# Larger loads in a ring of three slots for a decode-attention kernel whose time is set by its transfers

## The chip, the cores and the metric

The kernel runs on one core of one Trainium2 chip. The metric is the device time of a whole execution in microseconds (us). The time before is 402.05 us, the median of three runs (402.03 to 402.28).

In this text PE is the matrix engine, DVE the vector engine, ACT the scalar engine, POOL the general-purpose engine, and SP the engine that issues the large loads. "The 16 engines" are the 16 DMA engines of the core. Each large load is cut by rows (128 partitions, 8 rows per engine), and one packet is one contiguous run of one row.

## The reference

One token goes through attention with a long cache and, beside it, through a small MLP. All large data are bf16.

```python
x  = A_x                                  # (1, 1, 1024)
xn = layernorm(x)
# attention: 32 query heads, 4 KV heads, 65536 keys, Dh 128
q = xn @ wq                               # wq 1024 x 4096
scores = q . k_cache * Dh**-0.5           # k_cache, v_cache (1, 4, 65536, 128)
a = softmax(scores) @ v_cache
a = a.reshape(1, 1, 4096) @ wo            # wo 4096 x 1024
# MLP mixer on xn
h  = gelu(layernorm(xn) @ w1)             # w1 1024 x 1024
hs = (h, its four quarters shifted by 1 or 2 along the sequence) @ w2
x1 = xn + hs
h2 = gelu(layernorm(x1) @ w3) @ w4        # w3 1024 x 3584, w4 3584 x 1024
out = x + a + x1 + h2
```

The kernel reads 169.87 MB, of which K and V are 134.2 MB.

## The kernel before

K and V come in loads of 4 MB (16384 keys, 32 KB per partition), into two slots each. DVE transposes K from its slot into a buffer `X` in pieces of 32x32. The softmax runs over 8192 keys at a time (index `n`), and POOL keeps the running output. Weights share a buffer `W`, or borrow a slot.

```python
W = sb("W", [P, 14336], BF)
X = sb("X", [P, 2, 8192], BF)
Kn = sb("Kn", [P, 2, 16384], BF)
Vn = sb("Vn", [P, 2, 16384], BF)
# ... cut
def issue_kv(t, b_t, cache, m, ch):
    h, nb = divmod(m, NPAIR // HKV)
    s = m % 2
    src = cache[0, h, nb * 2 * SUB:(nb + 1) * 2 * SUB, :].rearrange("(p c) d -> p (c d)", p=P)
    _dma(q_sp, chan("%s%d" % (ch, s)), lambda e: e.dma_start(out=t[:, s, :], in_=src), writes=b_t[s])
# ... cut
def Ttr(n, idx):          # transposes of K, out of place: slot -> X
    s, half = (n // 2) % 2, n % 2
    for ix in idx:
        _op(q_dve, lambda e, ix=ix: e.transpose(out=X32[:, n % 2, 1024 * ix:1024 * (ix + 1)],
                in_=Kn32[:, s, 4096 * half + 1024 * ix:4096 * half + 1024 * (ix + 1)]), ...)
# ... cut
for n in range(NT):       # 32 groups of 8192 keys
    QK(n)
    Ttr(n + 1, [0])       # the next group's K is transposed while this group is worked on
    stats1(n); MB(n); stats2(n); EXP(n)
    Ttr(n + 1, [1])
    PTr(n)
    Ttr(n + 1, [2, 3])
    PV(n); FLASH(n)
    # ... weights: w1, w2, w3, wo, each in W
    if n % 2 == 0: issue_k(n // 2 + 2)
    else:          issue_v(n // 2 + 2)
# w4 comes last, in four loads of 14, 8, 4 and 2 rows per partition
```

The weights' products are made in between, and the last work after the last load is eight matmuls, one copy and a 2 KB store.

## Time and profile before

| | before |
|---|---|
| time, median of three | 402.05 us |
| span in the profile | 400.9 us |
| bytes read | 169.87 MB |
| packets in all | 7087 |
| busy: DMA queue q1 / DVE / PE | 98.6% / 57% / 49% |

The table of windows (columns: stretch, its length, busy time of five engines with instruction counts, PE's granted clock, DMA share, GB/s):

```profile
core 0: us, PE busy (x) PEld busy (x) DVE busy (x) ACT busy (x) POOL busy (x), PEclk, DMA share, GB/s
...
100.00:150.00 50.00, 26.34 (x283) 12.74 (x286) 29.88 (x56) 5.77 (x15) 6.98 (x9) 0.57 1.00 429
...
300.00:350.00 50.00, 24.75 (x208) 8.28 (x212) 34.96 (x55) 7.24 (x19) 7.41 (x9) 0.53 1.00 431
```

A DMA share of 1.00 means that the transfers never pause.

The end of the span, from the timeline (start us, us, engine, line, operation; in brackets the idle time before it and what ended that):

```profile
394.51 1.88 PE L404 MATMUL OUT_ps<-Kn,gh_bf 128*1 128x256 bf16 x32 [1.69 <-DMA Kn<-in_B_w_dram]
...
396.93 1.02 PE L404 MATMUL OUT_ps<-Kn,gh_bf 128*1 128x256 bf16 x16 [0.54 <-DMA Kn<-in_B_w_dram]
...
398.16 0.60 PE L404 MATMUL OUT_ps<-Kn,gh_bf 128*1 128x256 bf16 x8 [0.20 <-DMA Kn<-in_B_w_dram]
398.80 0.42 DVE L631 CAST orow<-OUT_ps 128x256 bf16<-128x256 f32 x1 [13.00 <-PE OUT_ps L404]
399.26 0.65 SPq L632 DMA_DIRECT2D out_dram<-orow  x1
```

The trace also has a record of every packet with start and duration. The medians before are 159 ns for 4 KB, 309 for 8 KB, 611 for 16 KB, 1062 for 28 KB and 1213 for 32 KB.

### The profile page before, as it was taken

How to read it: one execution, taken by the hardware profiler on the slowest of the kernel's cores; microseconds unless marked ns; L12 is line 12 of the kernel's file. 1: busy time of each engine (PE TensorE's matmuls, PEld its weight loads, DVE VectorE, ACT ScalarE, POOL GpSimd, SP SyncE). 2: the span in 40 equal slices, each digit the busy share in tenths (PEclk: the TensorE clock that was granted, in tenths of full speed). 3: DMA queues.
4: the chain of work that ended last, by engine and by line, in shares of the span. 5: the costliest groups of instructions: out<-in, count | busy, mean ns of one | idle time of the engine just before them, and what ended most of it. 6: DMA issues, size and time to landing. Idle time of an engine off the chain costs nothing.

```text
span 400.9 us, 4792 instructions
## 1 busy us (share of the span) xinstructions
PE 194.8 (49%) x1875; PEld 78.5 (20%) x1875; DVE 228.3 (57%) x401; ACT 48.9 (12%) x128; POOL 61.8 (15%) x90
## 2 busy tenths in 40 slices
PE   0432435064525756186541965464443755445655
PEld 0211111021103511062110731121101311111132
DVE  0247475376816588256745287576836775788310
ACT  1000111011101012011110011111201111121100
POOL 5000012012111012011210101111110112112110
PEclk9985656556565566555655555555555655585565
DMA  9999999999999999999999999999999999999994
GB/s 366 451 438 416 427 435 445 418 446 441 417 422 449 436 425 428 432 440 418 433 448 425 420 440 441 422 430 442 418 430 441 445 420 428 423 431 430 443 415 204
DMA packets 7087, 170.19 MB, mean 424 GB/s; under 512 B 916, under 2 KB 920, under 8 KB 1048
## 3 DMA queue, kind: packets, MB, share of 16 engines
q1 hardware_dynamic: 6920, 169.87, 98.6%
q8 instruction: 15, 0.25, 0.2%
q14 instruction: 8, 0.07, 0.0%
q10 hardware_dynamic: 144, 0.00, 0.0%
HBM read 169.87 MB, written 0.00 MB: 424 GB/s over the span
## 4 chain that ended last, share of the span: by engine, by line
DMA 55%; DVE 23%; PE 17%; ACT 2%; issue 2%; POOL 0%; SPq 0%; ACTq 0%
DMA Kn<-in_A_k_cache_dram 44%; DVE X L476 12%; DMA Kn<-in_B_w_dram 6%; DMA Vn<-in_A_wq_dram 5%; PE H_ps L366 4%; PE S_ps L488 3%; DVE pT_f L529 3%; PE OT_ps L536 3%; DVE mrow L495 3%; ACT p_sb L518 2%; PE PT_ps L527 2%; PE M_ps L366 1%; PE M_ps L564 1%; PE OUT_ps L404 1%; DVE Yall L393 1%
## 5 line engine op out<-in xcount | busy, mean ns | idle before, releaser
L476 DVE STREAM_TRANSPOSE X<-Kn 128x1024 f32<-128x1024 f32 x128 | 151.7, 1215 | 67.5 <-DMA Kn<-in_A_k_cache_dram 67.5
L536 PE MATMUL OT_ps<-Vn,pT_f 128*32 128x512 bf16 x512 | 60.7, 627 | 27.2 <-DVE pT_f L529 27.2
L488 PE MATMUL S_ps<-X,Yall 128*32 128x512 bf16 x512 | 58.9, 607 | 16.1 <-DVE X L476 16.1
L501 PE MATMUL MB_ps<-Rm,Lmat 128*128 128x16 bf16 x32 | 6.1, 191 | 90.4 <-DVE Rm L496 90.4
L550 POOL TENSOR_TENSOR O_acc<-O_acc,tmpO 128x513 f32<-128x513 f32 x28 | 32.9, 1174 | 88.4 <-ACT tmpO L544 88.4
L518 ACT ACTIVATE p_sb<-S_ps,brun 128x512 bf16<-128x512 f32 x32 | 22.0, 687 | 192.6 <-DVE brun L516 157.3
L548 POOL TENSOR_SCALAR O_acc<-O_acc,ff 128x513 f32<-128x513 f32 x28 | 19.5, 698 | 153.3 <-ACT ff L523 153.3
L527 PE MATMUL PT_ps<-p_sb,permR 128*128 128x512 bf16 x32 | 17.5, 548 | 38.6 <-ACT p_sb L518 38.6
L495 DVE TENSOR_REDUCE mrow<-S_ps 128x1 f32<-128x512 f32 x32 | 21.6, 674 | 25.5 <-PE S_ps L488 25.5
L544 ACT ACTIVATE tmpO<-OT_ps 128x512 f32<-128x512 f32 x32 | 19.1, 598 | 107.9 <-PE OT_ps L536 107.9
L488 PEld LDWEIGHTS S_ps<-X,Yall 128*32 128x32 bf16 x512 | 16.6, 126 | 54.7 <-DVE X L476 38.2
L529 DVE STREAM_TRANSPOSE pT_f<-PT_ps 128x512 f32<-128x512 f32 x32 | 22.9, 716 | 5.9 <-PE PT_ps L527 5.9
L536 PEld LDWEIGHTS OT_ps<-Vn,pT_f 128*32 128x32 bf16 x512 | 14.5, 129 | 59.0 <-DVE pT_f L529 41.9
L501 PEld LDWEIGHTS MB_ps<-Rm,Lmat 128*128 128x128 bf16 x32 | 3.2, 101 | 115.1 <-DVE Rm L496 115.1
L366 PEld LDWEIGHTS H_ps<-xn_bf,W 128*128 128x128 bf16 x224 | 14.4, 167 | 1.7 <-issue 1.7
L366 PE MATMUL H_ps<-xn_bf,W 128*128 128x1 bf16 x224 | 14.5, 202 | 0.0
L527 PEld LDWEIGHTS PT_ps<-p_sb,permR 128*128 128x128 bf16 x32 | 3.3, 104 | 41.4 <-ACT p_sb L518 41.4
L505 DVE TENSOR_REDUCE Bst<-MB_ps 128x1 f32<-128x16 f32 x32 | 5.5, 173 | 8.3 <-PE MB_ps L501 8.3
L330 PE MATMUL M_ps<-ln_s,ones_f 128*128 128x1 f32 x6 | 1.8, 363 | 16.6 <-DVE ln_s L329 16.6
L546 POOL COPY O_acc<-tmpO 128x513 f32<-128x513 f32 x4 | 2.5, 612 | 47.5 <-ACT tmpO L544 47.5
L404 PE MATMUL OUT_ps<-Kn,gh_bf 128*1 128x256 bf16 x112 | 6.7, 413 | 4.3 <-DMA Kn<-in_B_w_dram 4.3
L631 DVE CAST orow<-OUT_ps 128x256 bf16<-128x256 f32 x1 | 0.4, 425 | 13.0 <-PE OUT_ps L404 13.0
(109 smaller groups left out, 116.4 us busy)
## 6 DMA issues: line engine op xcount, KB each, us to landing
Kn<-in_A_k_cache_dram SPq DMA_DIRECT2D x15, 4096.0 KB, 27.7
Vn<-in_A_v_cache_dram SPq DMA_DIRECT2D x15, 4096.0 KB, 23.1
W<-in_B_w_dram SPq DMA_DIRECT2D x2, 3584.0 KB, 24.9
W<-in_A_wo_dram SPq DMA_DIRECT2D x3, 2048.0 KB, 24.1
Kn<-in_A_wq_dram SPq DMA_DIRECT2D x1, 4096.0 KB, 12.1
Vn<-in_A_wq_dram SPq DMA_DIRECT2D x1, 4096.0 KB, 20.9
W<-in_B_w_dram SPq DMA_DIRECT2D x2, 2048.0 KB, 33.9
Kn<-in_A_k_cache_dram SPq DMA_DIRECT2D x2, 2048.0 KB, 24.9
```

Of the source, the lines that this page charges most:

```text
L366: fns.append(lambda e, j=j, cx=cx: e.matmul(ps_tile[:, c0 + cx:c0 + cx + 1], lhs_fn(j - j0, cx), rhs_fn(j), start=(j == 0 and cx == 0), st ...
L404: fns.append(lambda e, lhs=lhs, rhs=rhs, jj=jj: e.matmul(OUT_ps[32 * jj:32 * jj + 1, 0:256], lhs, rhs[:, 256 * jj:256 * jj + 256], start=F ...
L476: _op(q_dve, lambda e, ix=ix: e.transpose(out=X32[:, xs, 1024 * ix:1024 * (ix + 1)], in_=Kn32[:, s, 4096 * half + 1024 * ix:4096 * half + ...
L488: fns.append(lambda e, we=we, cm=cm, mv=mv: e.matmul(S_ps[32 * cm:32 * cm + 32, :], Yall[:, h, we, :, :].rearrange("p a g -> p (a g)"), mv ...
L495: _op(q_dve, lambda e: e.reduce_max(mrow[:, m:m + 1], S_ps[:, :], axis=AX.X), reads=[b_S], writes=[b_mrow[m]])
L518: _op(q_act, lambda e: e.activation(p_sb[:, m, :], S_ps[:, :], ACTF.Exp, bias=brun[:, kn:kn + 1], scale=SCALE, accum_out=tmpO[:, m, 512:513]),
L527: _op(q_pe, lambda e: e.matmul(PT_ps[:, :], permR[:, :], p_sb[:, m, :], start=True, stop=True), reads=[b_p[m], b_const], writes=[b_PT])
L529: _op(q_dve, lambda e: e.transpose(out=pT_f[:, :], in_=PT_ps[:, :]), reads=[b_PT], writes=[b_pT])
L536: fns.append(lambda e, q=q, q4=q4: e.matmul(OT_ps[32 * q4:32 * q4 + 32, :], pT_bf[:, q, :, 1], Vn[:, s, 8192 * half + 512 * q:8192 * half ...
L544: _op(q_act, lambda e: e.activation(tmpO[:, m, 0:512], OT_ps[:, :], ACTF.Copy), reads=[b_OT], writes=[b_tmpO[m]], partial=True)
L548: _op(q_pool, lambda e: e.tensor_scalar(out=O_acc[:, :], in0=O_acc[:, :], scalar1=ff[:, m:m + 1], scalar2=0.0, op0=ALU.mult, op1=ALU.add), ...
L550: _op(q_pool, lambda e: e.tensor_tensor(out=O_acc[:, :], in0=O_acc[:, :], in1=tmpO[:, m, :], op=ALU.add), reads=[b_tmpO[m]], writes=[b_Oacc])
```

## The change

The intent is to make the large transfers cheaper by making them fewer: fewer packets and fewer loads for the same bytes. To make room, `X`, `W` and the four 32 KB slots become a ring of three slots of 64 KB per partition, K is transposed within its slot, and the small weights' vectors live in the unused end of a slot. A softmax group is 16384 keys, so POOL's running output goes away, and ACT and PE have fewer instructions. `wo` and `w4` are loaded last. The core of the diff, cut:

```diff
-        W = sb("W", [P, 14336], BF)
-        X = sb("X", [P, 2, 8192], BF)
-        Kn = sb("Kn", [P, 2, 16384], BF)
-        Vn = sb("Vn", [P, 2, 16384], BF)
+        KV = sb("KV", [P, 3, SLOT], BF)              # SLOT = 32768 elements = 64 KB
 ...
+        def kv_load(s, ch, src, n, bufs=None):
+            _dma(q_sp, chan(ch), lambda e: e.dma_start(out=KV[:, s, 0:n], in_=src), writes=b_KV[s] if bufs is None else bufs)
 ...
+        kv_load(0, "s0", rows_src(A_wq, 0, 8), 8 * HQD)      # then w1, w2 into slot 1, w3 into slot 2
+        def issue(i):                                # i = 3, 4, ...: K, V, K, V ... of 32768 keys
+                kv_load(slot(i), "s%d" % slot(i), src, SLOT)
 ...
-                _op(q_dve, lambda e, ix=ix: e.transpose(out=X32[...], in_=Kn32[...]), ...)
+                _op(q_dve, lambda e, o=o: e.transpose(out=KV32[:, s, o:o + 1024], in_=KV32[:, s, o:o + 1024]), ...)
 ...
-        w4_parts = [(0, 14, 0, 0), (14, 8, 1, 0), (22, 4, 1, 8), (26, 2, 0, 14)]
+        w4_parts = [(0, 17), (17, 7), (24, 3), (27, 1)]
 ...
+        for m in range(NBLK):                        # 8 blocks of 32768 keys, n = 4 * m
+            Ttr(n, range(4)); QK(n)
+            Ttr(n + 1, range(4)); QK(n + 1)
+            Ttr(n + 2, [0, 1]); MAX(2 * m); Ttr(n + 2, [2]); EXP(2 * m); Ttr(n + 2, [3]); QK(n + 2)
+            PT(n); Ttr(n + 3, [0]); PTr(n); PT(n + 1); Ttr(n + 3, [1]); PTr(n + 1); Ttr(n + 3, [2, 3])
+            PV(n); QK(n + 3)
+            issue(6 + 2 * m)                         # into the slot of this block's K
+            PV(n + 1); MAX(2 * m + 1); EXP(2 * m + 1); FLUSH(2 * m)
+            ...; PV(n + 2); PV(n + 3); FLUSH(2 * m + 1)
+            issue(7 + 2 * m)                         # into the slot of this block's V
```

Before, group n+1's K was transposed while group n was worked on; now a block's transposes begin in the block itself, after the work of the block before is done.

## The prediction

> **What bounds it now.** The transfers. The page's DMA line shows the 16 engines at 90% or more in 39 of 40 slices, and its queue part gives queue q1 98.6% of 16 engines' span: 169.87 MB at 424 GB/s. DVE is busy 57%, PE 49%, ACT 12%, POOL 15% of the span. In the table of windows the DMA share is 0.97 to 1.05 in every 10 us from 10 to 390, so no wait of the queue ever lets an engine run dry; the long SyncE waits (158 us on the PV matmuls) only delay issues that still come in time. The chain of waits agrees: 55% DMA.
>
> Packet records in the trace, medians: 159 ns for 4096 B, 309 for 8192, 611 for 16384, 1062 for 28672, 1213 for 32768. A line of about 27.2 B/ns per engine plus about 9 ns per packet. 16 engines x 27.2 = 435 GB/s; the Trainium skill, "DMA: Bandwidth & Descriptors", section "Where 436 GB/s comes from", states 435.2 GB/s, and the trace agrees. The floor of 169.87 MB is about 390 us. The rest: 6144 data packets x 9 ns / 16 = 3.5 us; 48 loads' closing semaphore writes (9 ns on each engine) 0.4 us; stretched packets 1.3 us; 1.0 us before the first packet; 3.2 us from the last weight byte to the end of the span; 1.1 us between span and reported time.
>
> **What the change does.** Bytes stay the same. Rows of 64 KB per partition halve most packets: 3200 data packets by my count (K, V, wq and wo 64 KB, w3 56 KB, w1 and w2 16 KB). Saved: 2944 x 9 ns / 16 = 1.7 us, plus 22 loads fewer, 0.2 us. The last piece of w4 is one row, so 4 closing matmuls instead of 8 (those 8 took 0.62 us): 0.1 to 0.2 us.
>
> Compute falls (pooled maximum and exponential, no POOL accumulation, wide projections), but none of it sets the time, so I count nothing.
>
> The risk: the ring has three slots of 8.4 MB, 19.3 us each. The K slot of a block is free once its 16 transposes (16 x 1.2 us), the first V matmuls and the last QK are done: an estimate of 25 us after K lands, against 38.7 us until the queue runs dry. The V slot is freed about 33 to 38 us after K lands, with 58 us allowed. In front, wq is used up by 27 us; w1 to w3 keep the queue full until 47; K0 lasts till 66, V0 till 86, and K1 waits only for the gelu, near 58. So no starvation.
>
> **Prediction.** 402.05 - 1.9 - 0.1 = 400.0 us; 399.0 to 401.9. Faster by over 2% (below 394.0) would need more than all of what lies above the byte floor that the change touches: 0.01. Same 0.96, slower 0.03.
>
> **Checks.** Packets fall to about 4000 in all with the 64 KB ones near 2417 ns (16 x 27.2 B/ns again); DMA share stays near 1.0 in each window from 10 to 390 us; last-slice tail unchanged; POOL under 5%, time unmoved by it.
>
> **Wrong if:** Packets split at 32 KB (then about 401.7); 64 KB rows reading memory slower, which shows as packets above 2417 ns; a hole in the DMA share because a slot is freed late, likeliest around the first blocks (40 to 90 us) or at the wo and w4 loads at the end.

## More of the kernel before

The sequence has one position, so each quarter of `h` is shifted out and zeros take its place: `hs` is zero whatever `w1` and `w2` hold.

From the page of the kernel before: busy time of each engine, the busy share of the 16 DMA engines in 40 slices of the span (in tenths), the DMA totals, the large loads' queue, and the chain of waits that ended last.

```profile
PE 194.8 (49%) x1875; PEld 78.5 (20%) x1875; DVE 228.3 (57%) x401; ACT 48.9 (12%) x128; POOL 61.8 (15%) x90
...
DMA  9999999999999999999999999999999999999994
...
DMA packets 7087, 170.19 MB, mean 424 GB/s; under 512 B 916, under 2 KB 920, under 8 KB 1048
...
q1 hardware_dynamic: 6920, 169.87, 98.6%
...
DMA 55%; DVE 23%; PE 17%; ACT 2%; issue 2%; POOL 0%; SPq 0%; ACTq 0%
...
x_bf<-in_A_x_dram ACTq DMA_DIRECT2D x1, 2.0 KB, 12.2
```

The DMA row is what counts: 9 in every slice but the last. No engine that computes is near that. The last line is a DMA issue of another kind: the small load of `x` (2 KB) took 12.2 us from its issue to its landing.

One more view gets its meaning only later, so it is recorded here: DVE's waits in the kernel before (who waited for whom: us in total, times, longest).

```profile
DVE X L476 <- DMA Kn<-in_A_k_cache_dram: 67.5, 11, 9.3
```

DVE stands still for 67.5 us because the next K has not landed yet. That is a first measure of the room that the compute has.

## The result, and the profile after

The changed kernel takes 402.32 us, the median of four runs (401.99 to 402.56). Its ratio to the kernel before is 1.0004 with a 95% interval from 0.9986 to 1.0021: the same. The class was expected, but it says little: the forecast gain of 2.0 us (0.5%) would have been "the same" too. The time lies outside the predicted range of 399.0 to 401.9, and the gain is missing.

The lines of the page after that answer to those of before:

```profile
PE 176.5 (44%) x1611; PEld 70.7 (18%) x1627; DVE 224.5 (56%) x347; ACT 25.2 (6%) x53; POOL 7.1 (2%) x30
...
DMA  9999899999999999999999999999999999999994
...
DMA packets 3770, 170.13 MB, mean 425 GB/s; under 512 B 548, under 2 KB 552, under 8 KB 808
...
q1 hardware_dynamic: 3608, 169.87, 98.4%
...
DMA 41%; DVE 30%; PE 23%; issue 3%; another core or an unknown queue 2%; POOL 0%; SPq 0%; ACT 0%; DVEq 0%
...
KV<-in_A_x_dram ACTq DMA_DIRECT2D x1, 2.0 KB, 22.2
```

The packets are nearly halved (7087 to 3770), POOL and ACT are nearly idle, and the rate over the span is the same 424 to 425 GB/s. The load of `x` lands 10 us later. The chain of waits has less DMA in it and more DVE and PE.

The windows after:

```profile
core 0: us, PE busy (x) PEld busy (x) DVE busy (x) ACT busy (x) POOL busy (x), PEclk, DMA share, GB/s
...
100.00:150.00 50.00, 19.55 (x164) 5.72 (x158) 30.89 (x40) 2.59 (x6) 0.00 (x0) 0.57 1.01 436
...
300.00:350.00 50.00, 19.50 (x158) 7.09 (x156) 32.64 (x42) 2.99 (x6) 0.00 (x0) 0.60 1.00 433
```

The DMA share is 1.00 again: no starvation. DVE's waits for K after:

```profile
DVE KV L436 <- DMA KV<-in_A_k_cache_dram: 8.7, 4, 3.8
```

The room of the compute has shrunk from 67.5 us to 8.7. The end of the span after:

```profile
395.29 0.93 PE L543 MATMUL S_ps<-KV,gh_bf 128*1 128x256 bf16 x28 [2.22 <-DMA KV<-in_B_w_dram]
...
397.18 0.81 PE L543 MATMUL S_ps<-KV,gh_bf 128*1 128x256 bf16 x12 [0.96 <-DMA KV<-in_B_w_dram]
...
398.16 0.38 PE L543 MATMUL S_ps<-KV,gh_bf 128*1 128x256 bf16 x4 [0.16 <-PE S_ps L543]
398.59 0.43 DVE L612 CAST orow<-S_ps 128x256 bf16<-128x256 f32 x1 [15.77 <-PE S_ps L543]
399.05 0.65 SPq L613 DMA_DIRECT2D out_dram<-orow  x1
```

From before to after the last landing of a weight byte moves from 398.11 to 397.80 us, and the store's issue from 399.26 to 399.05.

The packet records of the two traces, worked out:

| | before | after |
|---|---|---|
| K and V packets, data packets in all | 32 KB, 6144 | 64 KB, 3200 |
| their recorded duration, median (ns) | 1213 | 2421 (mean 2431) |
| packets of the same size, first 21 us (ns) | 1213 | 2418 |
| overlap: the next packet starts before the recorded end, by about (ns) | 3.4 | 3.4 |
| sum of all records of queue q1, over 16 engines (us) | 395.27 | 394.36 |
| last landing: earliest and latest of the 16 engines (us) | 394.45 to 398.11 | 394.61 to 397.80 |
| time for 8.39 MB of K or V in the steady stretch (us) | 19.36 | 19.36 |

The last row is the result in one number. Two packets of 32 KB take as long as one of 64 KB, to within 1 ns: an engine does 16 x 1209.6 ns (1213 less the overlap) or 8 x 2420 ns, both 19.36 us. The halved count did not pay, because what one packet costs beyond its bytes rose, by the first two sets of experiments to 1.7 times as much.

### The profile page after: what moved, and what is told of

The parts are those of the page before. It is cut to its first block, busy times and chain, and to the rows that moved or that the text cites. A ratio compares the mean times of both kernels' runs of the same rounds, so it can differ in the third digit from the quotient of the medians.

```text
span 400.7 us, 3966 instructions
## 1 busy us (share of the span) xinstructions
PE 176.5 (44%) x1611; PEld 70.7 (18%) x1627; DVE 224.5 (56%) x347; ACT 25.2 (6%) x53; POOL 7.1 (2%) x30
## 2 busy tenths in 40 slices
DMA packets 3770, 170.13 MB, mean 425 GB/s; under 512 B 548, under 2 KB 552, under 8 KB 808
## 3 DMA queue, kind: packets, MB, share of 16 engines
q1 hardware_dynamic: 3608, 169.87, 98.4%
HBM read 169.87 MB, written 0.00 MB: 424 GB/s over the span
## 4 chain that ended last, share of the span: by engine, by line
DMA 41%; DVE 30%; PE 23%; issue 3%; another core or an unknown queue 2%; POOL 0%; SPq 0%; ACT 0%; DVEq 0%
DMA KV<-in_A_k_cache_dram 29%; DVE KV L436 21%; PE S_ps L448 8%; DMA KV<-in_B_w_dram 7%; DMA KV<-in_A_x_dram 6%; PE OT_ps L492 5%; PE S_ps L385 3%; DVE pT_f L483 2%; PE M_ps L400 2%; DVE mrow L455 2%; PE S_ps L353 1%; PE M_ps L520 1%; DVE Yall L369 1%; PE PT_ps L479 1%
## 5 line engine op out<-in xcount | busy, mean ns | idle before, releaser
L436 DVE STREAM_TRANSPOSE KV<-KV 128x1024 f32<-128x1024 f32 x128 | 148.6, 1210 | 8.8 <-DMA KV<-in_A_k_cache_dram 8.7
L448 PE MATMUL S_ps<-KV,Yall 128*32 128x512 bf16 x512 | 60.7, 622 | 114.5 <-DVE KV L436 114.5
L492 PE MATMUL OT_ps<-KV,pT_f 128*32 128x512 bf16 x512 | 59.3, 612 | 1.3 <-PE OT_ps L492 1.3
L448 PEld LDWEIGHTS S_ps<-KV,Yall 128*32 128x32 bf16 x512 | 16.8, 125 | 148.0 <-DVE KV L436 132.2
L470 ACT ACTIVATE p_sb<-S_ps,brun 128x1024 bf16<-128x1024 f32 x16 | 17.8, 1115 | 281.0 <-DVE brun L468 177.3
L455 DVE TENSOR_REDUCE mrow<-S_ps 128x1 f32<-128x1024 f32 x16 | 19.5, 1216 | 16.8 <-PE S_ps L448 16.7
L479 PE MATMUL PT_ps<-p_sb,permR 128*128 128x512 bf16 x16 | 8.8, 553 | 37.2 <-DVE pT_f L483 37.2
L492 PEld LDWEIGHTS OT_ps<-KV,pT_f 128*32 128x32 bf16 x512 | 17.1, 132 | 35.0 <-issue 33.3
L505 DVE SCALAR_TENSOR_TENSOR O_acc<-O_acc,ff,OT_ps 128x512 f32<-128x512 f32 x12 | 8.9, 744 | 23.6 <-PE OT_ps L492 23.6
L385 PE MATMUL S_ps<-KV 128*32 128x512 bf16 x88 | 12.3, 549 | 2.9 <-DVE KV L333 2.9
```

The costliest lines, as they stand in the source:

```text
L385: fns.append(lambda e, j=j, k=k, mv=mv: e.matmul(S_ps[32 * (k % 4):32 * (k % 4) + 32, bank + k // 4, :], vec[:, j:j + 1].broadcast_to([P, ...
L436: _op(q_dve, lambda e, o=o: e.transpose(out=KV32[:, s, o:o + 1024], in_=KV32[:, s, o:o + 1024]), reads=[b_KV[s][4 * sub + ix]], writes=[b_ ...
L448: fns.append(lambda e, we=we, cm=cm, mv=mv: e.matmul(S_ps[32 * cm:32 * cm + 32, n % 4, :], Yall[:, h, we, :, :].rearrange("p a g -> p (a g ...
L455: _op(q_dve, lambda e: e.reduce_max(mrow[:, k:k + 1], S_ps[:, 2 * k:2 * k + 2, :].rearrange("p b c -> p (b c)"), axis=AX.X), reads=b_S[2 * ...
L470: _op(q_act, lambda e: e.activation(p_sb[:, :, :].rearrange("p b c -> p (b c)"), S_ps[:, 2 * k:2 * k + 2, :].rearrange("p b c -> p (b c)") ...
L479: _op(q_pe, lambda e: e.matmul(PT_ps[:, :], permR[:, :], p_sb[:, n % 2, :], start=True, stop=True), reads=[b_p[n % 2], b_const], writes=[b ...
```

## The experiments

18 kernels ran. They ask three things: what a packet costs in each kernel, what sets the end, and how far the compute is from setting the time.

### What a packet costs in the new kernel

Theory A: every packet has a toll of its own, so that the packet count sets the difference between the kernels. Theory B: only bytes count, and a packet's toll is hidden. `rows32` and `rows4` cut each large load into pieces of half a row (32 KB) and of 4 KB per partition, with nothing else changed. `after_again` repeats the changed kernel, with five rounds, on the same chip.

```diff
 def kv_load(s, ch, src, n, bufs=None):
-    _dma(q_sp, chan(ch), lambda e: e.dma_start(out=KV[:, s, 0:n], in_=src), ...)
+    for o in range(0, n, R):          # R = 16384 (rows32) or 2048 elements (rows4)
+        ... e.dma_start(out=KV[:, s, o:o + R], in_=src[:, o:o + R]) ...   # same semaphore
```

> The changed kernel once more, as the control for the other runs of this set and for the noise. Two theories of why the larger packets saved nothing. Theory A, the prediction's: every packet costs about 9 ns on its engine beyond its bytes, so 1.9 us were saved and lost again elsewhere (stretched packets, uneven engines, tail). Theory B: the 9 ns are an artefact of the packet records, which overlap by 3 to 4 ns at every change of packet; an engine moves 27.08 B/ns whatever the packet size from 32 KB to 64 KB (in both traces 8.39 MB land every 19.36 us in the steady stretch), so nothing was there to save. Both: 402.0 to 402.5 us, ratio to before 0.999 to 1.001. The last weights of the slowest engine land near 397.8, 3.2 us after those of the fastest one.

Measured: 401.75 us, ratio 0.9996 (0.9984 to 1.0009). This median is 0.6 us below the first one and inside the predicted range, but the ratio is again that of no change.

> The changed kernel with every load of 56 or 64 KB rows split into two transfers of half rows, so the packets are those of before and everything else is that of the change. 2432 more packets and 19 more transfers. Theory A: +1.5 us over the unsplit kernel. Theory B: 0 to +0.3 us. On the side: the small load of x, whose 8 packets per engine alternate with the big ones, should land near 12 us again instead of 22.

Measured: 403.29 us, ratio 1.0029 (1.0016 to 1.0043): 1.3 us more than the changed kernel in the same rounds by the ratios (0.0033 x 402). The steady stretch needs 19.45 us per 8.39 MB; the half-row packets take 1216 ns, and every fourth 1224, not the 1213 of the kernel before.

> The same split driven to pieces of 4 KB rows (w4 untouched): about 37000 more packets, 288 more transfers. Theory A: 37000 x 9 ns / 16 = 20.8 us and 2.6 us for the closing semaphore writes, so about +23 us. Theory B: from the 4 KB pieces at the end of the kernel before, which took 1.216 us for 0.524 MB against 1.210 at the flat rate, about +2 us, at most +4. x should land near 3.5 us.

Measured: 423.84 us, ratio 1.0536 (1.0522 to 1.055): 21.7 us more than the changed kernel in the same rounds (0.0540 x 402). The trace has 36,608 more data packets, and 41,184 more packets of the queue when the small closing writes of the more numerous loads are counted too. That is 21.7 us x 16 / 36608 = 9.5 ns per data packet, or 8.4 ns per packet of either kind. Theory B falls. Of theory A the toll holds; whether the toll is the same in both kernels is the next question.

### What a packet costs in the kernel before, and whether the chip makes the difference

The dearer packets of the changed kernel could have come from the chip on which it ran (theory C) or from the kernel itself (theory D). `before_again` runs the unchanged kernel once more; `b_rows4` cuts its 30 whole loads of K and V into 4 KB rows.

```diff
-    e.dma_start(out=t[:, s, :], in_=src)
+    for o in range(0, 16384, 2048): e.dma_start(out=t[:, s, o:o + 2048], in_=src[:, o:o + 2048])   # b_rows4
```

> The kernel before once more, as the control of this set. In its first trace a 32 KB packet took 1213 ns throughout; in the changed kernel with its loads cut to the same 32 KB, 3 of 4 engines took 1216 and 1 of 4 took 1224, from about 30 us on. Theory C: this belongs to the chip the run fell on, so this trace shows 1216 and 1224 as well. Theory D: something in the changed kernel causes it, and this trace shows 1213 again. 402.2 us in either case.

Measured: 402.06 us, ratio 1.0001; the packets are at 1213 ns again. (The expectation speaks of one engine in four at 1224 ns; the records do not name the engine, but chained by their start and end times they show about every fourth packet of each engine.) This run alone could not settle theory C, because it fell on another chip (1) than `rows32` (7). The other runs do: on chip 1 the changed kernel's variants `pe_less` and `pe_more` have 2421 ns, and on chips 3 and 6 too its variants have the surplus while those of the kernel before (`b_dve`, `b_low`) have 1213. Theory C falls.

> The kernel before with its 30 undivided K and V loads cut into 8 pieces of 4 KB rows: 26880 more packets, 210 more transfers, nothing else. Cutting the loads of the changed kernel to 4 KB cost 21.8 us for 37000 packets, 9.4 ns each. If that toll holds in any kernel: 26880 x 9.4 / 16 = +15.8 us. If packets are cheaper in the kernel before (theory D: 3 to 5 ns less each), +8 to +11 us. If packets cost nothing here (theory B), below +3 us.

Measured: 411.28 us, ratio 1.0229 (1.0216 to 1.0243): 9.2 us for 26,880 more data packets (30,240 with the closing writes). That is 5.5 ns per data packet, or 4.9 ns per packet of either kind. The data packets are flat at 159 ns. The large loads' queue on the pages of `rows4` and `b_rows4`:

```profile
q1 hardware_dynamic: 44792, 169.89, 100.6%
...
q1 hardware_dynamic: 37160, 169.89, 100.3%
```

So, counted the same way, a packet costs 1.7 times as much in the new kernel (8.4 over 4.9). The prediction had read 9 ns from the durations; the records overlap by about 3.4 ns, and 9 less 3.4 is close to the 5.5 that was measured. In the new kernel the records are longer by a further amount that hardly depends on the packet's size: after 50 us, leaving out packets stretched by more than 20 ns, the mean is 3.9 ns above 159 for 4 KB (`rows4`), 4.8 above 1213 for 32 KB (`rows32`) and 4.3 above 2418 for 64 KB (`after`). So it is a surplus per packet and not slower reading of long rows, and 5.5 + 3.9 = 9.4 ns is the 9.5 that `rows4` measured.

### Why the packets are dearer in the new kernel

The surplus shows first 31 to 35 us into the changed kernel (28 us in `rows32`, about 16 in `rows4`), and it never shows in any variant of the kernel before. Five more theories were tried, and all fell.

`runs32` (theory F: the rows of neighbouring partitions lie 64 KB apart in memory) takes a block as two contiguous runs of 4 MB, each into half a slot, so K and V are read as before. `shift32` (theory G: the slots start on a multiple of 4096 bytes) moves the ring by 256 bytes. `pool32` (theory H: POOL is idle) gives POOL eight copies per block. `shift32` and `pool32` are on top of `rows32`.

```diff
+    src = cache[0, h, nb * BLK + o * (BLK // 2):..., :]   # runs32: two loads, each from its own 4 MB run
-    pad = 28672 - nc.sbuf_base
+    pad = 28416 - nc.sbuf_base                            # shift32
+    8 x POOL tensor_copy(O_acc -> scratch) in each block  # pool32
```

> The changed kernel, but each 8 MB K or V block comes as two transfers that each read one contiguous 4 MB run, 32 KB per partition, as the kernel before reads them; the keys of a block are thereby dealt to partitions in another order, alike for K and V, so the result stays right. wq, w3, wo and w4 unchanged. 2048 more packets than the unsplit kernel. Theory F: what makes a packet dearer in the changed kernel (1216 and 1224 ns for 32 KB against 1213) is the distance of 64 KB between the rows of neighbouring partitions in memory. Then the 32 KB packets take 1213 ns here, and the time is within 0.3 us of the unsplit kernel's. If the distance has nothing to do with it: 1216 and 1224 ns as in the split by half rows, 1.3 us slower than the unsplit kernel, about 403.3 us.

Measured: 403.19 us, ratio 1.0031 (1.0018 to 1.0043), packets at 1216 and 1224 ns.

> The half-row split with the ring moved by 256 bytes, to partition offset 28416, so that its slots no longer start at multiples of 4096, as in the kernel before. Theory G: packets are dearer because of where they land. Then 1213 ns throughout. If not, 1216 and 1224 as before the move.

Measured in one look: 403.31 us, packets at 1216 and 1224 ns.

> The half-row split with 8 idle copies of the accumulator on POOL at the end of each block, so that POOL works on through the run as it did before the change. Theory H: a POOL that only waits disturbs the transfers. Then packets fall back to 1213 ns after the first block, near 90 us. If not, 1216 and 1224 throughout.

Measured in one look: 403.8 us, packets at 1216 and 1224 ns, with POOL busy for 46.4 us. F falls, and so do G and H as far as one run each, of this one shift and these copies, can tell.

`no_ttr` leaves the transposes of K out, but for the first four (theory I: DVE rewriting the slots makes packets dearer). `b_low` puts the K buffer of the kernel before where its weights lay (theory J: the address in the partition).

```diff
-    for ix in idx:
+    for ix in idx if n == 0 else ():                      # no_ttr
+    Kn = sb("Kn", [P, 2, 16384], BF)                      # b_low: allocated before W and X
     W = sb("W", [P, 14336], BF)
```

> The new kernel without the transposes of K in place (only four of the first group kept), so wrong result on purpose. DVE loses 124 transposes of 1.2 us, about 150 us of its 224 us busy, and no longer rewrites the ring's slots. Account so far (the transfers set the time): 0 to -0.5 us, that is 0.998 to 1.001 of the kernel before. If DVE's 30% in the chain of waits were time that bounds: down by tens of us. Theory I (DVE's rewriting of the slots makes the large packets dearer): the 64 KB packets stay at 2418 ns through the whole run, and the time falls by about 0.8 us; otherwise the pattern 2421, 2421, 2421, 2428 comes back.

Measured: 401.86 us, ratio 0.9992 (0.9977 to 1.0007). The pattern of 2421, 2421, 2421, 2428 ns comes back unchanged. Theory I falls. The kernel is wrong by construction; the comparison with the reference passed all the same, so this check does not see an error in the weights of the softmax.

With the transposes gone, DVE no longer holds PE up, and every V and seven of the eight K are waited for. PE's waits in this run:

```profile
PE OT_ps L492 <- DMA KV<-in_A_v_cache_dram: 68.0, 8, 10.5
PE S_ps L448 <- DMA KV<-in_A_k_cache_dram: 45.9, 7, 7.0
```

This run has a second use: it takes 139 us off DVE's busy time (224.5 to 85.9), and its median lies 0.5 us below the first median of the changed kernel and 0.1 above the second. The missing 1.9 us are therefore not compute.

> The kernel before with the K buffer allocated first of the large ones, so that its 64 KB lie where the weights lay (from byte 36608), and W and X behind it. Theory J (where in the partition the data land makes packets dearer): the K packets rise above 1213 ns for part of the run. Otherwise 1213 ns flat, and the time within 0.5 us of the kernel before.

Measured in one look: 402.14 us, beside 402.21 for the kernel before. The packets stay at 1213 ns from start to end. Theory J falls too, as far as this one move of the K buffer can tell. What makes the packets dearer stays open. One hint is in the trace of `dve4` below: once its queue had run dry for the first time, shortly before 187 us, most packets were back at 2418 ns (101 of 135 between 200 and 220 us). But the surplus can leave without that: in `after` 143 of the 2090 packets of 64 KB after 60 us took 2418 ns, on a few engines at a time, while the queue never ran dry; in `after_again` it was 1 of 2092. So, as far as packets can be put down to engines by their times, it is a state that a single engine can be in or out of, and what sets it was not found.

### What sets the end

The 16 engines finish their last share at different times: over 3.66 us before and 3.19 us after. The packet records show how this arises. Whenever a 16 KB packet of PE's instruction fetch (queue q8; 15 of them before, 13 after) falls on an engine, that engine's lead or lag moves by about 1.2 us, and no later load evens it out, since every load gives each engine the same share. Theory E: fewer fetches mean an earlier end, more fetches a later one. `pe_less` drops half of the score matmuls and three quarters of the output matmuls (wrong result); `pe_more` adds 1024 matmuls of one column.

```diff
-    for we in range(4):            # QK
+    for we in range(2):            # pe_less; in PV: for q in range(4)
+    128 x matmul(M_ps[:, 500:501], permR, sel16[:, 0:1])  # pe_more, after the last FLUSH of each block
```

> The changed kernel with a wrong result on purpose: 2 of the 4 QK matmul groups and 4 of the 16 PV matmuls per sub-block, 640 fewer matmuls and as many weight loads; loads and waits unchanged. Theory E: PE's instructions are fetched in 16 KB packets, 13 in the changed kernel, and each delays one of 8 engines by about 1.3 us, two per engine on five of them; the slowest engine sets the end. With 1958 instead of 3238 PE instructions there are 8 fetches, one per engine: the spread of the last landings falls from 3.2 to about 1.8 us and the time by 1.2 to 1.4 us. If the compute chain (DVE 30% and PE 23% in the chain of waits) set the pace, over 5 us faster. If neither, unchanged.

Measured: 401.58 us, ratio 0.9987 (0.9975 to 1.0), with 8 fetches. The spread of the last landings is 3.29 us: one engine still came 1.3 us after the second-latest, which was 2.02 us after the earliest. The landings load by load show why: the engine that was already the latest, by 2.3 us, met the fetch at 321 us and was 3.3 us behind from then on. The expected gain did not come.

> The changed kernel with 128 one-column matmuls that nobody reads at the end of each block, 1024 in all: 2048 more PE instructions. Theory E: 8 more fetches, 21, so at least one engine meets three: spread 4.5 us or so, 1.2 to 1.5 us slower. If only PE's time mattered: the added 9 us per block delay the next block, whose V load was issued only 4 to 11 us before the queue would have run dry, so holes in the DMA share and well over 5 us slower. If neither, unchanged.

Measured: 403.67 us, ratio 1.0038 (1.0026 to 1.0051). Its fetch queue on the page:

```profile
q8 instruction: 21, 0.34, 0.3%
```

The last landing is at 399.38 us instead of 397.80, the spread 4.76 us, and there is no hole in the DMA share. The adding side of theory E is confirmed. On the taking side no gain was shown: one engine with bad luck was enough to keep the end where it was.

`tail` cuts the closing loads of `w4` differently, so that fewer matmuls wait for the last-but-one piece.

```diff
-    w4_parts = [(0, 17), (17, 7), (24, 3), (27, 1)]
+    w4_parts = [(0, 17), (17, 8), (25, 2), (27, 1)]
```

> The changed kernel with w4 split in 17, 8, 2 and 1 rows instead of 17, 7, 3 and 1. In its trace the last row had landed near 397.8 us but the 12 matmuls of the 3-row piece kept PE until 398.1. With 8 matmuls in front the last 4 should start near 397.9: 0.2 to 0.3 us faster than the unsplit kernel. If PE was not what held the end, no change.

Measured: 402.11 us, ratio 1.0002 (0.9989 to 1.0014): no gain that the runs can tell. In its trace the last landing is at 398.04 us and PE had only just finished the second piece: its 32 matmuls took from 396.15 to 398.02, so the 12 matmuls of the last two pieces still followed.

### How far the compute is from setting the time

The prediction held that no compute sets the time in either kernel. `dve4` and `dve2` add four and two transposes to each of the 8 blocks of the changed kernel, of pieces that are transposed anyway. In `dve4` the expectation still rested on the queue running ahead.

```diff
             Ttr(n, range(4))
+            Ttr(n, [0, 0])            # dve4 and dve2: 2 x 1.21 us per block
...
             Ttr(n + 1, range(4))
+            Ttr(n + 1, [0, 0])        # dve4 only
```

> The new kernel with four more transposes per block, of the same pieces, before the right ones, wrong result on purpose (a piece transposed three times is transposed once in effect, so it may even come out right). 32 x 1.2 us = 38 us more work for DVE. Account so far: 0 to +1 us, since K slots still come free before the queue runs dry. If the chain's 30% of DVE were time that bounds: +38 us or a large part of it.

Measured: 428.0 us, ratio 1.0636 (1.0618 to 1.0654): 25.8 us more than the kernel before. This expectation missed by far. Its windows now have holes (the DMA share is the last column but one):

```profile
core 0: us, PE busy (x) PEld busy (x) DVE busy (x) ACT busy (x) POOL busy (x), PEclk, DMA share, GB/s
...
150.00:200.00 50.00, 18.34 (x142) 6.62 (x144) 34.05 (x43) 2.99 (x6) 0.00 (x0) 0.56 0.90 384
200.00:250.00 50.00, 18.20 (x150) 5.55 (x152) 38.98 (x48) 2.59 (x6) 0.00 (x0) 0.57 0.98 420
250.00:300.00 50.00, 19.84 (x156) 6.50 (x158) 36.38 (x44) 2.99 (x6) 0.00 (x0) 0.53 0.88 377
```

DVE is busy for only 34 to 39 us of each 50, and still its chain sets the pace. The share of busy time hides this, because DVE and PE wait for each other within a block. The right reading was DVE's wait for K, 8.7 us in all. The timeline of the unchanged `after` shows where it stood in the steady stretch (first transposes of a block that had to wait for K):

```profile
224.65 4.62 DVE L436 STREAM_TRANSPOSE KV<-KV 128x1024 f32<-128x1024 f32 x4 [0.69 <-DMA KV<-in_A_k_cache_dram]
...
302.10 4.62 DVE L436 STREAM_TRANSPOSE KV<-KV 128x1024 f32<-128x1024 f32 x4 [0.59 <-DMA KV<-in_A_k_cache_dram]
```

The two are one KV head apart, 77.45 us, in which DVE waited for K 0.59 us. The other 76.9 us are a chain of DVE, PE and ACT. So two clocks run almost equally fast: the transfers need 77.4 us per head, and the compute chain 76.9. The traces of `dve2` and `dve4` bear this out: with 4 and 8 more transposes per head, 76.9 us become 81.7 and 86.6, and from the second head on their heads begin 81.0 to 81.9 and 86.2 to 87.4 us apart.

This gave theory K: DVE's 8.7 us of waits and about 4.3 us of bytes still queued when a V load is issued are free, 13.0 us in all, and what goes beyond is paid in full. It fits `dve4` (38.8 - 13.0 = 25.8) but was formed from it, so it was put to a new test against rival L, a price of two thirds for each transpose. Beside it `b_dve` puts about as much into the kernel before (31 transposes; DVE is busy 37.2 us longer).

```diff
             Ttr(n + 1, [0])
+            Ttr(n + 1, [0])           # b_dve: in 31 of the 32 groups of the kernel before
```

> The new kernel with two more transposes per block (16 x 1.21 = 19.4 us of DVE; result right, since a piece transposed three times is transposed once). Theory K (the new kernel's work on a block is one chain of DVE and PE that fills the time of its two loads but for little: DVE waited for K only 8.7 us in all, and a V load is issued with as little as 4.1 us of bytes still queued): the first 8.7 + 4.3 = 13 us are free and the rest is paid, so +6.4 us (+4 to +9); the same sum gives +25.8 for 38.8 us, which is what four more cost. Rival L (every added transpose is paid at two thirds of its time, because it disturbs the loads): +13 us.

Measured: 408.68 us median, ratio 1.0177 (1.0141 to 1.0213; one of the four runs, at 411.23, lifts the mean; whether it is slower by 2% is unclear). That is 6.4 us over the kernel before by the medians of the same rounds, and 7.1 by the ratio. Theory K said 6.4, rival L 13. DVE's wait for K is used up:

```profile
DVE KV L436 <- DMA KV<-in_A_k_cache_dram: 0.7, 1, 0.7
```

> The kernel before with one more transpose per group of 8192 keys (31 x 1.25 = 38.8 us of DVE, as much as the four per block in the new kernel; result right, since it writes the same once more). Theory K: DVE waits for K there 67.5 us in all, so nothing is paid: -0.3 to +1 us. Rival L: about +26 us, as in the new kernel.

Measured: 401.85 us, ratio 0.999 (0.9975 to 1.0005): nothing is paid. Its DVE still waits for K:

```profile
DVE X L476 <- DMA Kn<-in_A_k_cache_dram: 47.0, 10, 7.4
```

The bytes still queued on SP's ring when each V load is issued, over 434 GB/s, tell the same story. It is worked out from issue times and packet records, in us:

| V load of block | 1 | 2 | 3 | 4 | 5 | 6 | 7 |
|---|---|---|---|---|---|---|---|
| after | 11.4 | 11.9 | 4.7 | 8.3 | 4.1 | 8.3 | 4.6 |
| dve2 | 7.9 | 9.1 | 2.2 | 4.6 | 0.0 | 3.5 | 0.0 |
| dve4 | 5.4 | 4.5 | 0.0 | 0.6 | 0.0 | 0.8 | 0.0 |

Every second block is tighter, because it also closes a KV head. Where a number is zero, the transfers had run dry.

### What the bytes are worth

`nofeed` leaves out the loads of `w1` and `w2` and the work on them; the result stays right, since with one position their share is zero. `best` adds the cut of `tail`.

```diff
-    kv_load(1, "w1", rows_src(B_w1, 0, 8), 8 * D, b_w1)
-    _dma(q_sp, chan("w2"), ... in_=rows_src(B_w2, 0, 8) ...)
...
-    proj(1, 0, D, xn2_bf, 2, ...); gelu(...); proj(1, 8 * D, D, g_bf, 3, ...)
-    x1 = xn + ...; acc = acc + ...
+    _op(q_dve, lambda e: e.tensor_copy(x1, xn), reads=[b_xn], writes=[b_x1])
```

> The changed kernel without loading w1 and w2: for a sequence of one, the shifted h is all zeros whatever w1 is, so h's product with w2 is zero, and the kernel multiplied w2 by a zero vector already. Same result. 4.19 MB less at 433 GB/s: 9.7 us faster, 392.4 us. If anything but the bytes set the time, less.

Measured: 392.24 us, ratio 0.975 (0.9736 to 0.9763). The queue carried 165.68 MB instead of 169.87:

```profile
q1 hardware_dynamic: 3320, 165.68, 98.3%
```

The changed kernel itself did not run in these rounds. Against its two medians, 402.32 and 401.75 us, 4.19 MB less took 10.1 or 9.5 us off; at the 433 GB/s of the steady stretch (8.39 MB in 19.36 us) it would be 9.7.

> The new kernel without the loads of w1 and w2 and the work on them (result correct), with the closing loads of w4 cut 17, 8, 2, 1 rows instead of 17, 7, 3, 1. Expected about the same as without the tail's new cut: 392.2 us, 0.975; the finer tail is worth 0 to -0.3 us, less than the runs tell apart.

Measured: 392.08 us, ratio 0.9753 (0.9738 to 0.9768), no different from `nofeed`. These two beat both kernels, and by fewer bytes alone.

## Why the prediction was right or wrong

- Right: the transfers set the time, and nothing starves. The DMA share is 1.0 in the windows before and after, and taking away bytes changed the time at about the transfer rate (`nofeed`: 9.5 to 10.1 us, where that rate gives 9.7), while taking 139 us of work from DVE did not (`no_ttr`).
- Right, as far as the runs can tell: the fall in POOL, ACT and PE work moved nothing.
- Right: packets fell to about 4000 (3770), and a packet of 64 KB is not split.
- **Wrong, and the step that failed:** "6144 data packets x 9 ns / 16 = 3.5 us" and, from it, "Saved: 2944 x 9 ns / 16 = 1.7 us". Two errors lie in the one term. First, the 9 ns were read from recorded durations as if packets followed each other end to end; they overlap by 3.4 ns, and the toll measured in the kernel before is 4.9 to 5.5 ns (`b_rows4`). Secondly, the toll was taken to be the same in the new kernel, where it is 8.4 to 9.5 ns (`rows4`). As an estimate with the tolls per packet of either kind, q1's packets paid 6920 x 4.9 / 16 = 2.1 us before and pay 3608 x 8.4 / 16 = 1.9 us now: a gain of 0.2 us where the prediction had 1.9 for packets and loads.
- In terms of the sums: the records of queue q1 fell by 0.9 us, not by 1.9. Of these, about 3300 fewer overlaps of 3.4 ns take back 3300 x 3.4 / 16 = 0.7 us, so that about 0.2 us of real time remains. Of the 1.0 us by which the records fell short, 0.6 us is the surplus of the large packets over the 2418 ns of the first 21 us: the 2251 of the 2304 that nothing stretched average 4.1 ns above it, and 2304 x 4.1 ns / 16 = 0.6 us. The rest was not followed up. The reason for the surplus is open; chip, row distance and in-place transposes are ruled out, and the start address of the ring, idle POOL and the place of the K buffer as far as one look at each can do that.
- The prediction had named the sign of it: "64 KB rows reading memory slower, which shows as packets above 2417 ns". The sign came, but not for the reason named, since packets of 4 KB have the surplus too. A median of 2421 ns looks harmless next to 2417; over 2304 packets it is not.
- The tail was mis-sized: 0.1 to 0.2 us from four closing matmuls instead of eight. The closing matmuls did fall from 0.60 to 0.38 us. But the last landing came 0.31 us earlier and the store only 0.21, because the 12 matmuls of the piece before kept PE from 397.18 to 397.99; from the last landing to the store's issue it took 1.15 us before and 1.25 after. When the end falls depends on the slowest of 16 engines, and a shift of one of PE's instruction fetches moves that by 1.2 us (`pe_more`: 1.6 us later).
- The floor was set too low: 169.87 MB at 435 GB/s is 390 us. At the 433 GB/s that the steady stretch shows, it is 392 us. The Trainium skill, "DMA: Bandwidth & Descriptors", section "Where 436 GB/s comes from", gives 435.2 GB/s as the ceiling; the trace agrees, with 433 GB/s including the packets' tolls.
- "So no starvation" was right with far less room than the text implied. It estimated 33 to 38 us for freeing a V slot against "58 us allowed", and 25 us for a K slot against 38.7. From K's landing to the issue of the load into its slot it took 25 us in the first two blocks and 29 to 33 in the next five. The new K or V load was issued with as little as 4.1 us of bytes left in the queue, and the whole compute chain stood 0.6 us per 77.4 from setting the pace. `dve2` and `dve4` show the edge; `b_dve` shows that the kernel before was far from it. The change gave away 59 us of DVE's wait for K (67.5 to 8.7), and with it most of the kernel's slack, for nothing.
- In front, the load of `x` landed 22.2 us after its issue instead of 12.2, so the query projection began at 28.0 us and K0 was issued at 33.5 instead of the predicted 27. The Trainium skill, "DMA: Bandwidth & Descriptors", section "Queues, rings and completion order", says that an engine goes round its queues by whole packets, each typically of 9 to 17 descriptors. The trace agrees on the round, with shorter turns: each engine has 8 small packets of `x`, and after each of them one large packet of one row goes first (8 x 1.21 = 9.7 us or 8 x 2.42 = 19.4 us, plus the first). With 4 KB rows (`rows4`) the same load landed 3.8 us after its issue. The delay cost nothing here, since the weights kept the queue full.

## What to carry to other kernels

When a kernel is bound by its transfers, halving the packets is worth what a packet costs beyond its bytes; measure that by cutting the loads finer and dividing the added time by the added packets, not from the lengths of overlapping records, and measure it in the kernel that you are going to. Before saying that compute is off the critical path, look at how long it waits for the data in each round, not at its share of busy time: here DVE was 57% and 56% busy, yet DVE waited 67 us for K in one kernel and 9 in the other. What does pay in such a kernel is to read fewer bytes.

## What the Trainium skill lacked or had wrong

- "DMA: Bandwidth & Descriptors", section "Where 436 GB/s comes from": it says without a condition that for transfers between memory and SBUF the memory side binds at about 358 GB/s per core; the same page says further up that this is what each of two busy cores of a pair gets, and that condition belongs here too. On the one core here such loads run at 433 GB/s in the steady stretch, close to the page's ceiling of 435.2.
- The same page, section "Why small descriptors are slow (HBM only)": it names a fixed overhead of about 3 cycles per packet and says that joining descriptors into packets is only worth it for descriptors of up to 256 B. The runs show 5.5 ns per data packet in one kernel (rows of 32 KB cut to 4 KB) and 9.5 ns in another (64 KB to 4 KB), where 4 KB rows instead of 64 KB rows cost 21.7 us. That the toll depends on the kernel is on no page, and its cause is open.
- The same page, section "Queues, rings and completion order": the round by whole packets is there, but not what it means for a small load beside large ones: 2 KB landed after 3.8 us beside 4 KB packets, 12.2 us beside 32 KB, and 22.2 us beside 64 KB.
- "Runtime: NRT & Kernel Launch", section "Instruction fetch mechanics": it says that instructions are refilled in blocks of 16 KiB over a DMA queue and that this is mostly hidden. The trace agrees on the size (15 packets before, 13 after). It is not hidden when the transfers bind: each puts its engine back by about 1.2 us for good, and the last landings of the 16 engines are 3.2 to 3.7 us apart at the end.
- No page gives a way to read how near compute is to setting the pace in a kernel that is bound by its transfers. Here the wait of DVE for its data did it: a kernel with 67.5 us of wait took 37.2 us of added work at no cost, one with 8.7 us paid 25.8 us for 38.8.
